# Column sums of three weight groups on GpSimd, one mean product each, and another order of the opening's splits and statistics

## The chip, the cores and the metric

The kernel runs on one core of one Trainium2 chip. A core has a matrix engine (TensorE; PE in the profile, its weight loads PEld), three engines that work element by element (VectorE = DVE, ScalarE = ACT, GpSimd = POOL) and a queue engine (SyncE = SP) that issues most of the transfers between the chip's memory and the core's on-chip memory, SBUF. Products are summed in PSUM, in eight banks. Each engine works through its own list of instructions in order and waits at semaphores for the others. The metric is the device time of one execution in microseconds; lower is better.

## The reference, cut to what matters

```python
x = A_u                                   # 1 x 2048 x 448, float32
g = sigmoid((x * gate_w).sum(-1))         # a gate per token
a = s4d_convolution(x, ...) + x * D_skip  # branch A
# branch B: a shift mixer, then an MLP
h  = gelu(layernorm(x) @ w1)              # 448 x 448
hs = shifted_by_1_-1_2_-2(h) @ w2         # four channel groups of 112, each shifted along the tokens
x1 = x + hs
b  = x1 + gelu(layernorm(x1) @ w3) @ w4   # 448 -> 1792 -> 448
out = g * a + (1 - g) * b
```

Only `layernorm(x) @ w1` for the first 512 tokens, and what follows from it, is touched by the change. The layernorm is rewritten: `layernorm(x) @ w1 = r * (x @ (w1 - column means of w1))`, where `r` is one over the standard deviation of a token. So the kernel subtracts from every column of `w1` that column's mean over the 448 inputs, multiplies, and scales the result by `r` afterwards.

## The kernel before, in words

The 2048 tokens are cut into 4 blocks of 512 (`NB`, `TB`). A unit is one group of output channels for one block: 16 units of kind "a" (the mixer; per block the four 112-channel groups of `w1`, in the order 0, 2, 1, 3), then 56 of kind "d" (the MLP; 14 per block). A unit has a first product `first(n)` into a PSUM bank, an activation, and a second product `second(n)` that adds into four banks `acc0` to `acc3`, one for each 128 tokens.

All products are in float32 by splitting: a value is a rounded high part (`xh`, `w1h`, `w2h`, `uh`), made by a ScalarE copy, and a low part (`xl`, `w1l`, `w2l`, `ul`), made by a VectorE subtraction. A product is then three: high by high, high by low, low by high. A `first` has 11 matmuls (four 128-row pieces of the 448 inputs, the last of which holds 64 high and 64 low rows), a `second` has 12.

The order of all work is written by hand: inside `tc.manual_schedule()` each engine does its instructions in the order in which the code calls them. `begin()` (line 780) is the opening: everything from the start up to the second product of unit 3. After it comes a loop over the units with tables of what is done at which unit.

What the opening calls:

- `constants()` fills small tiles on GpSimd, among them `cm`, a column of 1/448. `first_loads()` issues the transfers: `w1` group 0 and group 2 on ACT's queue, `x` of the first block (`x0`, a left and a right half of the 512 tokens), group 1, the rows of `x` for the statistics, then group 3, and later the identity `idt`, `w2` and the next block on SP's queue.
- `warm_up(m)` issues `m` products of zeros on TensorE.
- `presum(0)` gives the means of group 0: VectorE adds pieces 0 and 1 of the group into `ws`, and three float32 products with the broadcast column `cm` (64 rows of piece 3, piece 2, then `ws`) leave the mean of every column in a bank `pm`, the same in all 128 partitions. `col_means(g)` does it for the groups 2, 1 and 3 with four products and no addition, the fourth over the 64 rows of piece 3. A float32 product shows as two records in the profile.
- `center(g)` subtracts `pm` from the weights `w1r` in place (VectorE); `hi(*s1(g))` and `lo_(*s1(g))` then split them into `w1h` and `w1l`; `s2(g)` stands for the same of `w2`.
- `x_hi`, `x_lo` split the first block's `x`: `lh` is its left half, `rh` its right; `split_hi(1, ...)`, `split_lo(1, ...)` those of the second block. `c0`, `c1` are the left and right 256 output columns of unit 0.
- `stats_act(j)`, `stats_b(j0, j1)` give mean and variance of 128 tokens on ScalarE or VectorE; `rstd` is eleven short VectorE instructions from the variance to `r1`; `rstd_rows` transposes `r1` on TensorE (one product for each 128 tokens) and copies it to the rows `rb` on ScalarE.
- `act_mul(n)` (VectorE) scales unit n by `rb`; `act_head(n)` (ScalarE) is the GELU and the copy `uh`; `act_tail(n)` (VectorE) gives `ul`.

Of the kernel before, what the change touches and what calls it, by code (L numbers as in the profile page):

```python
# [17 lines left out]
D = 448  # L18
# [156 lines left out]
def mixer_and_small_steps(ctx, tc, xs, gg, okm, x, xT, xb, x0, w1, w2, w3, w4, par, logdt, dskip, ident, out):  # L175
# [9 lines left out]


    idt = big.tile([128, 128], F32, name="idt")
    cm = big.tile([128, 1], F32, name="cm")
    rt = big.tile([128, 1], F32, name="rt")
    rb = wk.tile([128, L + 2 * HALO + 8], F32, name="rb", tag="rb", bufs=1)  # L190
    warm = big.tile([128, 2 * TB], mybir.dt.bfloat16, name="warm", tag="yt")
# [77 lines left out]

    def constants():  # L270
        nc.gpsimd.memset(warm[:, :TB], 0.0)
        nc.gpsimd.memset(cm, 1.0 / D)
        nc.gpsimd.memset(one, 1.0)
        nc.gpsimd.memset(nu, 0.0)
        nc.gpsimd.memset(zero, 0.0)
        nc.gpsimd.memset(carry, 0.0)
        nc.gpsimd.memset(rb[:, 0:HALO], 0.0)
        nc.gpsimd.memset(rb[:, L + HALO:L + 2 * HALO], 0.0)
# [201 lines left out]
    def second(n):  # L480
        kind, b, i = units[n]
        if kind == "a":
            wh, wl, m = w2h[:, i, :], w2l[:, i, :], G
            s, e = i == 0, i == 3
        else:
            wh, wl = W4[i]
            m = 128
            s, e = i == 0, i == NF - 1
        for j in range(NT):
            if s:  # L490
                ACC[j] = ps.tile([128, D], F32, name=f"acc{j}", tag=f"acc{j}", bufs=1)
        q = [(j, p) for p in range(3) for j in range(NT)]
        if s or e:
            q.sort()
        for j, p in q:
            t = slice(j * 128, (j + 1) * 128)
            nc.tensor.matmul(ACC[j], (UL if p == 2 else UH)[n][:m, t], wl if p == 1 else wh,  # L497
                             start=s and p == 0, stop=e and p == 2)
# [197 lines left out]
        return pm[g]  # L696


    def col_means(g):
        p = mean_bank(g)  # L700
        for k in range(4):
            r = 64 if k == 3 else 128
            nc.tensor.matmul(p, cm[:r].to_broadcast([r, 128]), w1r[:r, g, k, :G],  # L703
                             start=(k == 0), stop=(k == 3))

    w4p, w3r = {}, {}

# [25 lines left out]
        for _ in range(m):  # L733
            nc.tensor.matmul(pw, warm[:, 0:128], warm[:, :TB], start=True, stop=True)  # L734

    def presum(g, m=1):

        t = big.tile([128, G], F32, name="ws", tag="lt")
        a, p = w1r[:, g, :, :G], mean_bank(g)
        nc.vector.tensor_add(t, a[:, 0, :], a[:, 1, :])  # L740
        if m > 1:
            nc.vector.tensor_add(t, t, a[:, 2, :])
        if m > 2:
            nc.vector.tensor_add(t[:64], t[:64], a[:64, 3, :])
        q = ((64, a[:64, 3, :]), (128, a[:, 2, :]))[:3 - m] + ((128, t),)
        for k, (r, q_) in enumerate(q):
            nc.tensor.matmul(p, cm[:r].to_broadcast([r, 128]), q_, start=(k == 0), stop=(k == 3 - m))  # L747

    def center(g, k0=0, k1=4):
        t = w1r[:, g, k0:k1, :G]  # L750
# [6 lines left out]
    def lo_(h, lo, src):  # L757
        nc.vector.tensor_tensor(lo, src, f32(h), OP.subtract)
# [21 lines left out]
    def begin():  # L780
        constants()
        first_loads()
        nc.scalar.activation(rt, cm, AF.Gelu_apprx_tanh)
        hl_tiles(("a", 0))
        warm_up(8)
        x_hi(0, lh)
        presum(0)
        center(0, 0, 2)
        center(0, 2, 4)
        warm_up(4)  # L790
        hi(*s1(0, 0, 2))
        x_lo(0, 2, lh)
        hi(*s1(0, 2, 4))
        x_hi(2, lh)
        first(0, seq=[(0, x_, k, *c0) for x_ in range(2) for k in range(2)], stop=False)
        col_means(2)
        lo_(*s1(0))
        first(0, seq=[(1, 0, k, *c0) for k in range(2)], stop=False)
        x_lo(3, 4, lh)
        x_lo(2, 3, lh)  # L800
        first(0, seq=[(w, 0, k, *c0) for k in (2, 3) for w in range(2)] + [(0, 1, 2, *c0)], stop=False)
        center(2)
        x_hi(2, rh)
        x_hi(0, rh)
        x_lo(3, 4, rh)
        hi(*s1(2))
        x_lo(2, 3, rh)
        first(0, seq=[(w, 0, k, *c1) for k in (2, 3, 0, 1) for w in range(2)], stop=False)
        x_lo(0, 2, rh)
        first(0, seq=[(0, 1, k, *c1) for k in (2, 0, 1)])  # L810
        col_means(1)
        lo_(*s1(2))
        first(1, seq=wh_wl)
        center(1)
        stats_act(2)
        stats_act(3)
        hi(*s1(1))
        stats_b(0, 2)
        col_means(3)
        stats_b(NT, NT + 1)  # L820
        hi(*s2(0))
        split_hi(1, 0, 2)
        first(2, seq=wh_wl[:7], stop=False)
        rstd(r1, 0, NT + 1)
        center(3)
        hi(*s1(3))
        rstd_rows(0, NT, "acc1")
        lo_(*s1(1))
        first(2, seq=wh_wl[7:])
        first(3, "misc", wh_wl[:7], stop=False)  # L830
        act_mul(0)
        lo_(*s1(3))
        first(3, seq=wh_wl[7:])
        lo_(*s2(0))
        act_head(0)
# [182 lines left out]
```

## Time and profile before

| what | value |
|---|---|
| three timed runs | 381.64, 382.9 and 383.3 us, median 382.9 |
| span of the profiled execution | 381.7 us |
| TensorE weight loads, busy | 318.3 us, 83% |
| VectorE busy | 294.9 us, 77% |
| ScalarE busy | 210.2 us, 55% |
| GpSimd, first work after the constants | at 49.08 us |
| 14 to 20 us: TensorE, VectorE, ScalarE busy | 6.00, 4.77, 2.99 of 6.00 us |
| 20 to 27 us: the same | 6.92, 5.12, 5.76 of 7.00 us |
| 38 to 93 us: the same | 54.45, 44.93, 29.76 of 55.00 us |

Times are counted from the start of the profiled execution, whose own time is its span with a little before and behind it that the profile does not hold. TensorE is busy nearly all the time, so its short gaps matter, and among them those in the first 40 us, where the change lies. In the chain of waits a piece of TensorE means that the engine had work in its list without a wait; a piece of another engine means that something waited for that.

### The profile page before, as it was taken

What the parts mean: (1) busy time and instruction counts of PE and PEld (TensorE: products, weight loads), DVE (VectorE), ACT (ScalarE), POOL (GpSimd) and SP (SyncE); (2) the same over time, 40 slices, a digit from 0 to 9 for tenths busy, and PEclk for the clock granted to TensorE, in tenths of its full rate; (3) what the DMA queues carried; (4) which work ended last, traced back from release to release, by engine and by line L of the source; (5) the groups of instructions that cost most, each with busy time, mean ns of one, the idle gap of its engine ahead of it and who ended that gap; (6) DMA issues with size and microseconds to landing.
All of it is one profiled execution on the core that took longest, in us unless ns stands there. A gap on an engine that the chain in (4) does not pass through costs nothing.

```text
span 381.7 us, 5198 instructions
## 1 busy us (share of the span) xinstructions
PE 373.2 (98%) x1728; PEld 318.3 (83%) x1728; DVE 294.9 (77%) x527; ACT 210.2 (55%) x349; POOL 65.3 (17%) x176
## 2 busy tenths in 40 slices
PE   8999999999999999999999999999999999999993
PEld 4878888887888888888888888888888888888882
DVE  3679988785866992888389999999788999995312
ACT  4575646636878566743275576465756745442220
POOL 1000061412000000030022536334142440000000
PEclk9999999999999999999999999999999999999998
DMA  8934505354724409000762614355785212271202
GB/s 268 371 99 184 193 29 154 48 102 142 257 87 128 73 16 216 32 0 0 194 131 43 117 28 106 95 173 110 108 186 152 60 21 35 57 198 31 82 0 101
DMA packets 85896, 42.26 MB, mean 111 GB/s; under 512 B 67030, under 2 KB 80614, under 8 KB 85226
## 3 DMA queue, kind: packets, MB, share of 16 engines
q1 hardware_dynamic: 85434, 41.20, 41.8%
q10 hardware_dynamic: 432, 0.70, 0.6%
q8 instruction: 15, 0.25, 0.3%
q14 instruction: 15, 0.12, 0.1%
HBM read 30.86 MB, written 11.02 MB: 110 GB/s over the span
## 4 chain that ended last, share of the span: by engine, by line
PE 92%; DVE 2%; DMA 2%; SPq 1%; ACT 0%; issue 0%; POOL 0%; DVEq 0%; POOLq 0%
PE p L435 45%; PE acc L497 44%; DMA raw<-w_in 2%; PE pw L734 1%; PE pm L703 1%; SPq L398 1%; DMA xd<-xt 1%; PE pm L747 0%; DVE b L284 0%; PE misc L334 0%; DVE w1r L751 0%; DVE w3l L218 0%; SPq L395 0%; DVE uf L444 0%; DVE ul L470 0%
## 5 line engine op out<-in xcount | busy, mean ns | idle before, releaser
L457 ACT ACTIVATE uf<-p 128x512 f32<-128x512 f32 x56 | 33.4, 597 | 102.9 <-PE p L435 102.9
L470 DVE TENSOR_TENSOR ul<-uf,uh 128x512 fp32r<-128x512 f32 (+1 forms) x72 | 48.8, 680 | 32.9 <-ACT uh L466 32.8
L620 DVE TENSOR_TENSOR_SCAN z<-z,carry 128x512 f32<-128x512 f32 x48 | 61.4, 1280 | 3.7
L435 PE MATMUL p<-xh,w3l 128*128 128x512 f32 x224 | 61.0, 393 | 0.6 <-DVE w3l L218 0.6
L435 PE MATMUL p<-xh,w3h 128*128 128x512 f32 x224 | 61.3, 396 | 0.0
L497 PE MATMUL acc<-w4h,uh 128*128 128x448 f32 x224 | 58.2, 364 | 0.0
L497 PE MATMUL acc<-w4h,ul 128*128 128x448 f32 x224 | 58.1, 364 | 0.0
L497 PE MATMUL acc<-w4l,uh 128*128 128x448 f32 x224 | 58.1, 363 | 0.0
L435 PEld LDWEIGHTS p<-xh,w3l 128*128 128x128 f32 x224 | 42.0, 188 | 10.8 <-DVE w3l L218 1.0
L435 PE MATMUL p<-xl,w3h 128*128 128x512 f32 x168 | 48.0, 394 | 0.0
L435 PEld LDWEIGHTS p<-xh,w3h 128*128 128x128 f32 x224 | 42.0, 188 | 6.7
L497 PEld LDWEIGHTS acc<-w4h,uh 128*128 128x128 f32 x224 | 42.0, 188 | 6.1
L466 ACT ACTIVATE uh<-uf 128x512 fp32r<-128x512 f32 (+1 forms) x72 | 45.5, 633 | 2.3
L497 PEld LDWEIGHTS acc<-w4l,uh 128*128 128x128 f32 x224 | 42.0, 188 | 3.2
L497 PEld LDWEIGHTS acc<-w4h,ul 128*128 128x128 f32 x224 | 42.0, 188 | 3.1
L615 ACT ACTIVATE z<-zs,nu 128x512 f32<-128x512 f32 x64 | 42.2, 709 | 0.7 <-DMA zs<-xT_in 0.7
L435 PEld LDWEIGHTS p<-xl,w3h 128*128 128x128 f32 x168 | 31.6, 188 | 7.2
L614 POOL COPY z<-carry 128x1 f32<-128x1 f32 x48 | 34.5, 731 | 17.2 <-DVE zs L626 17.1
L321 POOL TENSOR_TENSOR t<-r 128x4 f32<-128x4 f32 (+1 forms) x15 | 5.7, 377 | 149.1 <-DVE r L319 148.3
L622 POOL COPY carry<-z 128x1 f32<-128x1 f32 x48 | 14.2, 295 | 91.4 <-DVE z L620 89.8
L454 ACT ACTIVATE uf<-uf 112x512 f32<-112x512 f32 x16 | 10.1, 630 | 22.6 <-DVE uf L444 22.5
L620 DVE TENSOR_TENSOR_SCAN z<-z,carry,zero 128x512 f32<-128x512 f32 x16 | 20.0, 1247 | 0.0
(136 smaller groups left out, 488.8 us busy)
## 6 DMA issues: line engine op xcount, KB each, us to landing
zs<-xT_in SPq DMA_DIRECT2D x4, 1024.0 KB, 8.2
yd<-yt SPq DMA_DIRECT2D x56, 64.0 KB, 2.0
ysb<-yd SPq DMA_DIRECT2D x16, 224.0 KB, 2.6
out_dram<-xs SPq DMA_DIRECT2D x16, 224.0 KB, 2.4
raw<-xb_in SPq DMA_DIRECT2D x3, 1032.0 KB, 5.8
raw<-w_in SPq DMA_DIRECT2D x3, 1024.0 KB, 5.3
xd<-xt SPq DMA_DIRECT2D x16, 192.0 KB, 2.1
xr<-xd SPq DMA_DIRECT2D x16, 192.0 KB, 3.7
```

What stands on the lines that cost most here:

```text
L321: eng.tensor_mul(t, y, y)
L398: nc.sync.dma_start(p[o:o + 64, 3, :].rearrange("p (t c) -> p t c", c=32), d[384 * 128:].rearrange("(g p c) -> p g c", p=64, c=32))
L435: nc.tensor.matmul(p[:m, t0:t1], (wl if w else wh)[:, k, :], (xl if x_ else xh)[:, k, o + t0:o + t1], start=(q == 0 and fresh), stop=stop ...
L454: nc.scalar.activation(UF[n][:m], UF[n][:m], AF.Gelu_apprx_tanh)
L457: nc.scalar.activation(UF[n][:m], P1[n][:m], AF.Gelu_apprx_tanh)
L466: nc.scalar.activation(UH[n][:m], UF[n][:m], AF.Copy)
L470: nc.vector.tensor_sub(UL[n][:m], UF.pop(n)[:m], f32(UH[n][:m]))
L497: nc.tensor.matmul(ACC[j], (UL if p == 2 else UH)[n][:m, t], wl if p == 1 else wh, start=s and p == 0, stop=e and p == 2)
L614: nc.gpsimd.tensor_copy(z4[:, m, 0:1], carry[:, k, m:m + 1])
L615: nc.scalar.activation(z4[:, m, 1:], ZS[b][:, k, :], AF.Copy, scale=nu[:, k, m:m + 1])
L620: nc.vector.tensor_tensor_scan(z, z, up, carry[:, k, m:m + 1], OP.add, OP.add)
L622: nc.gpsimd.tensor_copy(carry[:, k, m:m + 1], z[:, TB - 1:])
```

## The change: what it does

```diff
-    cm = big.tile([128, 1], F32, name="cm")
+    cm = big.tile([128, 2], F32, name="cm")
...
-        nc.gpsimd.memset(cm, 1.0 / D)
+        nc.gpsimd.memset(cm[:, 0:1], 1.0 / D)
+        nc.gpsimd.memset(cm[:64, 1:2], 1.0 / D)
+        nc.gpsimd.memset(cm[64:, 1:2], 0.0)
...
         q = [(j, p) for p in range(3) for j in range(NT)]
-        if s or e:
+        if s and n or e:
             q.sort()
...
+    PS = []
+    def pool_sum(g):
+        if not PS:
+            PS.append(wk.tile([128, 4, G], F32, name="wsum", tag="u"))
+        t, a = PS[0][:, g], w1r[:, g, :, :G]
+        nc.gpsimd.tensor_add(t, a[:, 0, :], a[:, 1, :])
+        nc.gpsimd.tensor_add(t, t, a[:, 2, :])
+        nc.gpsimd.tensor_add(t[:64], t[:64], a[:64, 3, :])
+
     def col_means(g):
-        p = mean_bank(g)
-        for k in range(4):
-            r = 64 if k == 3 else 128
-            nc.tensor.matmul(p, cm[:r].to_broadcast([r, 128]), w1r[:r, g, k, :G],
-                             start=(k == 0), stop=(k == 3))
+        nc.tensor.matmul(mean_bank(g), cm[:, 0:1].to_broadcast([128, 128]), PS[0][:, g], start=True, stop=True)
...
-    def presum(g, m=1):
+    def presum():
         t = big.tile([128, G], F32, name="ws", tag="lt")
-        a, p = w1r[:, g, :, :G], mean_bank(g)
+        a, p = w1r[:, 0, :, :G], mean_bank(0)
         nc.vector.tensor_add(t, a[:, 0, :], a[:, 1, :])
...
-        q = ((64, a[:64, 3, :]), (128, a[:, 2, :]))[:3 - m] + ((128, t),)
-        for k, (r, q_) in enumerate(q):
-            nc.tensor.matmul(p, cm[:r].to_broadcast([r, 128]), q_, start=(k == 0), stop=(k == 3 - m))
+        for q, (c, r) in enumerate(((1, a[:, 3, :]), (0, a[:, 2, :]), (0, t))):
+            nc.tensor.matmul(p, cm[:, c:c + 1].to_broadcast([128, 128]), r, start=q == 0, stop=q == 2)
...
     def begin():
         constants()
         first_loads()
...
         warm_up(8)
         x_hi(0, lh)
-        presum(0)
+        presum()
+        for g in (2, 1, 3):
+            pool_sum(g)
+        x_hi(2, lh)
+        x_lo(0, 2, lh)
+        warm_up(3)
         center(0, 0, 2)
         center(0, 2, 4)
-        warm_up(4)
         hi(*s1(0, 0, 2))
-        x_lo(0, 2, lh)
         hi(*s1(0, 2, 4))
-        x_hi(2, lh)
-        first(0, seq=[(0, x_, k, *c0) for x_ in range(2) for k in range(2)], stop=False)
-        col_means(2)
-        lo_(*s1(0))
-        first(0, seq=[(1, 0, k, *c0) for k in range(2)], stop=False)
         x_lo(3, 4, lh)
         x_lo(2, 3, lh)
-        first(0, seq=[(w, 0, k, *c0) for k in (2, 3) for w in range(2)] + [(0, 1, 2, *c0)], stop=False)
+        first(0, seq=[(0, x_, k, *c0) for x_ in range(2) for k in range(2)], stop=False)
+        lo_(*s1(0))
+        first(0, seq=[(0, 0, 2, *c0), (0, 0, 3, *c0), (0, 1, 2, *c0)] + [(1, 0, k, *c0) for k in range(4)], stop=False)
+        col_means(2)
         center(2)
...
-        first(0, seq=[(w, 0, k, *c1) for k in (2, 3, 0, 1) for w in range(2)], stop=False)
+        first(0, seq=[(w, 0, 2, *c1) for w in range(2)] + [(w, 0, k, *c1) for k in (0, 1, 3) for w in range(2)], stop=False)
         x_lo(0, 2, rh)
         first(0, seq=[(0, 1, k, *c1) for k in (2, 0, 1)])
+        lo_(*s1(2))
         col_means(1)
-        lo_(*s1(2))
         first(1, seq=wh_wl)
         center(1)
         stats_act(2)
+        hi(*s1(1))
         stats_act(3)
-        hi(*s1(1))
         stats_b(0, 2)
+        lo_(*s1(1))
         col_means(3)
         stats_b(NT, NT + 1)
-        hi(*s2(0))
-        split_hi(1, 0, 2)
-        first(2, seq=wh_wl[:7], stop=False)
-        rstd(r1, 0, NT + 1)
         center(3)
         hi(*s1(3))
+        split_hi(1, 0, 2)
+        hi(*s2(0))
+        first(2, seq=wh_wl)
+        rstd(r1, 0, NT + 1)
+        first(3, "misc", wh_wl[:7], stop=False)
         rstd_rows(0, NT, "acc1")
-        lo_(*s1(1))
-        first(2, seq=wh_wl[7:])
-        first(3, "misc", wh_wl[:7], stop=False)
+        rstd_rows(NT, NT + 1, "acc2")
+        lo_(*s1(3))
         act_mul(0)
-        lo_(*s1(3))
         first(3, seq=wh_wl[7:])
...
         second(0)
-        rstd_rows(NT, NT + 1, "p1")
         act_mul(2)
```

Three things change in the list of the engines. On TensorE, in the stretch from the means of group 1 to the second product of unit 0 (`p_202`, `p_240`, `p_274` are the banks of units 1, 2 and 3, `misc` that of the transposes of `r_82`, which is `r1`), there stood before:

```order
L703 MATMUL pm<-w1r,cm 128x112 x4
L435 MATMUL p_202<-xh,w1h 112x512 x4
L435 MATMUL p_202<-xl,w1h 112x512 x3
L435 MATMUL p_202<-xh,w1l 112x512 x4
L435 MATMUL p_240<-xh,w1h 114x512 x4
L435 MATMUL p_240<-xl,w1h 114x512 x3
L334 MATMUL misc<-idt,r_82 128x128 x4
L435 MATMUL p_240<-xh,w1l 114x512 x4
L435 MATMUL p_274<-xh,w1h 112x512 x4
L435 MATMUL p_274<-xl,w1h 112x512 x3
L435 MATMUL p_274<-xh,w1l 112x512 x4
L497 MATMUL acc_309<-w2h,uh 128x448
```

The same stretch in the changed kernel, where the three banks are called `p_207`, `p_245` and `p_270`:

```order
L713 MATMUL pm<-wsum,cm 128x112
L437 MATMUL p_207<-xh,w1h 112x512 x4
L437 MATMUL p_207<-xl,w1h 112x512 x3
L437 MATMUL p_207<-xh,w1l 112x512 x4
L437 MATMUL p_245<-xh,w1h 114x512 x4
L437 MATMUL p_245<-xl,w1h 114x512 x3
L437 MATMUL p_245<-xh,w1l 114x512 x4
L437 MATMUL p_270<-xh,w1h 112x512 x4
L437 MATMUL p_270<-xl,w1h 112x512 x3
L336 MATMUL misc<-idt,r_82 128x128 x5
L437 MATMUL p_270<-xh,w1l 112x512 x4
L499 MATMUL acc_314<-w2h,uh 128x448
```

Each group's four mean products are one (that of group 3 stands between units 1 and 2 in both), and the transposes stand behind seven matmuls of unit 3, no longer behind seven of unit 2; the fifth transpose, which came after `second(0)`, has joined the four.

On VectorE, the stretch from the low part of group 2's weights to the scaling of unit 0 (`b` and `st` are the statistics, `w1r<-w1r,pm` is `center`) was before:

```order
L758 TENSOR_TENSOR w1l<-w1r,w1h 128x456
L751 TENSOR_TENSOR w1r<-w1r,pm 128x4x112
L284 BN_STATS b_222<-xs 128x6 x2
L286 BN_AGGR st<-b_222 128x2 x2
L284 BN_STATS b_232<-xs 128x6
L286 BN_AGGR st<-b_232 128x2
L299 TENSOR_SCALAR v<-st 128x5
...
L308 SCALAR_TENSOR_TENSOR r_82<-t,r_82 128x5
L751 TENSOR_TENSOR w1r<-w1r,pm 128x4x112
L758 TENSOR_TENSOR w1l<-w1r,w1h 128x456
L444 TENSOR_TENSOR uf<-p_158,rb 112x512
```

and is now:

```order
L762 TENSOR_TENSOR w1l<-w1r,w1h 128x456
L755 TENSOR_TENSOR w1r<-w1r,pm 128x4x112
L286 BN_STATS b_227<-xs 128x6 x2
L288 BN_AGGR st<-b_227 128x2 x2
L762 TENSOR_TENSOR w1l<-w1r,w1h 128x456
L286 BN_STATS b_235<-xs 128x6
L288 BN_AGGR st<-b_235 128x2
L755 TENSOR_TENSOR w1r<-w1r,pm 128x4x112
L301 TENSOR_SCALAR v<-st 128x5
...
L310 SCALAR_TENSOR_TENSOR r_82<-t,r_82 128x5
L762 TENSOR_TENSOR w1l<-w1r,w1h 128x456
L446 TENSOR_TENSOR uf<-p_171,rb 112x512
```

The low part of group 1 and the centering of group 3 have moved ahead of the eleven instructions of `rstd`.

GpSimd had nothing to do between its constants and the instructions of the later `rstd`; it now has, behind the constants (`ISA` sets up the engine):

```order
L280 MEMSET rb 128x2
L708 ISA
L708 TENSOR_TENSOR wsum<-w1r 128x112
L709 TENSOR_TENSOR wsum<-wsum,w1r 128x112
L710 TENSOR_TENSOR wsum<-wsum,w1r 64x112
```

and the same three additions twice more, for groups 1 and 3: nine additions that came from nowhere, in place of nine TensorE products.

More of the change, by code (lines that the diff above doesn't have):

```diff
@@ L734, in warm_up @@
             nc.tensor.matmul(pw, warm[:, 0:128], warm[:, :TB], start=True, stop=True)
-    def presum(g, m=1):
+    def presum():
         t = big.tile([128, G], F32, name="ws", tag="lt")
-        a, p = w1r[:, g, :, :G], mean_bank(g)
+        a, p = w1r[:, 0, :, :G], mean_bank(0)
         nc.vector.tensor_add(t, a[:, 0, :], a[:, 1, :])
[L741 to L744, printed above, removed]
-        q = ((64, a[:64, 3, :]), (128, a[:, 2, :]))[:3 - m] + ((128, t),)
-        for k, (r, q_) in enumerate(q):
-            nc.tensor.matmul(p, cm[:r].to_broadcast([r, 128]), q_, start=(k == 0), stop=(k == 3 - m))
+        for q, (c, r) in enumerate(((1, a[:, 3, :]), (0, a[:, 2, :]), (0, t))):
+            nc.tensor.matmul(p, cm[:, c:c + 1].to_broadcast([128, 128]), r, start=q == 0, stop=q == 2)
     def center(g, k0=0, k1=4):
@@ L782, in begin @@
         first_loads()
-        nc.scalar.activation(rt, cm, AF.Gelu_apprx_tanh)
+        nc.scalar.activation(rt, cm[:, 0:1], AF.Gelu_apprx_tanh)
         hl_tiles(("a", 0))
```

## The prediction

> **What bounds the kernel now.** I read the page's busy shares first, then the chain of work that ended last, then the opening in order of time.
>
> ```profile
> PE 373.2 (98%) x1728; PEld 318.3 (83%) x1728; DVE 294.9 (77%) x527; ACT 210.2 (55%) x349; POOL 65.3 (17%) x176
> PE 92%; DVE 2%; DMA 2%; SPq 1%; ACT 0%; issue 0%; POOL 0%; DVEq 0%; POOLq 0%
> ```
>
> TensorE is the bound. All that is changed lies before 28 us, and no transfer is moved past another. The chain there, and the one later place where it leaves TensorE:
>
> ```profile
> 9.29 1.65 PE pm L703 x8
> ...
> 13.66 1.07 PE pm L703 x8
> ...
> 14.75 0.62 DVE w1r L751
> ...
> 20.20 0.55 DVE w1l L758
> ...
> 20.79 3.71 PE p L435 x15
> ...
> 40.33 2.53 PE p L435 x11
> ...
> 75.52 0.34 PE misc L334 x3
> ...
> 92.67 1.42 PE p L435 x5
> ```
>
> From 14.75 to 20.79 the chain runs over VectorE while TensorE is busy too: the two are level, so TensorE's time alone isn't what the change can win. The stall before 92.67 follows a TensorE transpose at 75.52, so it moves with it: what the opening wins by 38 us reaches the end.
>
> **The change, part by part.** The rows of the opening:
>
> ```profile
> 4.83 1.46 PE L747 MATMUL pm<-w1r,cm 64*128 64x112 f32 x4
> 6.09 0.64 PE L747 MATMUL pm<-ws,cm 128*128 128x112 f32 x2
> 6.52 1.92 PE L734 MATMUL pw<-warm 128*128 128x512 bf16 x4
> 8.66 0.63 PE L435 MATMUL p<-xl,w1h 128*114 128x256 f32 x2
> 9.08 1.86 PE L703 MATMUL pm<-w1r,cm 128*128 128x112 f32 x8
> 10.98 0.62 DVE L751 TENSOR_TENSOR w1r<-w1r,pm 128x448 f32<-128x448 f32 x1 [1.46 <-PE pm L703]
> 11.63 0.42 DVE L776 TENSOR_TENSOR xh<-raw,xh 64x256 fp32r<-64x256 f32 x1
> 12.08 1.03 DVE L778 TENSOR_TENSOR xl<-raw,xh 128x256 fp32r<-128x256 f32 x2
> 13.03 0.63 DVE L758 TENSOR_TENSOR w1l<-w1r,w1h 128x456 fp32r<-128x456 f32 x1
> 14.64 1.18 PE L435 MATMUL p<-xh,w1h 128*112 128x512 f32 x4
> 17.28 1.22 PE L703 MATMUL pm<-w1r,cm 128*128 128x112 f32 x8
> 18.43 1.17 PE L435 MATMUL p<-xh,w1h 128*114 128x512 f32 x4
> ```
>
> 1. *Group 0's means.* Six half products lie between 4.83 and 6.52, 1.69 us. Two of 128 rows start 0.21 apart (6.09, then 6.52 after two). Six without 64-row passes: 1.29. Gain 0.4. One warm-up product less: four start in 8.44 - 6.52 = 1.92, about 0.43 each with the last one's tail taken off. Unit 0's first product, two ahead of 8.66 and so at 8.23, comes at 8.23 - 0.83 = 7.4 to 7.5.
>
> 2. *Group 2's mean.* It came after 4 products of unit 0; now it comes after 11, at 0.21 each (two from 8.66 to 9.08): 7.45 + 2.3 = 9.8. It is then 2 half products, not 8 (1.86). `center(2)`, which waits for it, starts at about 10.45 where it started at 10.98: 0.5 earlier. Its four followers on VectorE (11.63 to 13.66) are the same, so the last of unit 0's products, which need them, end 0.5 earlier too.
>
> 3. *Groups 1 and 3.* The mean of group 3 takes 18.43 - 17.28 = 1.15 for 8 half products; one product is 0.22. Gain 0.93, twice. `first(1)`, at 14.64, starts at 13.2; `first(2)`, at 18.43, at about 15.95.
>
> 4. *The transposes.* These now stand behind 18 matmuls from there, 0.23 each (11 in 2.53): 15.95 + 4.14 = 20.1. Where they stood:
>
> ```profile
> 19.50 0.17 DVE L308 SCALAR_TENSOR_TENSOR r<-t,r 128x5 f32<-128x5 f32 x1
> 20.11 0.60 PE L334 MATMUL misc<-idt,r 128*128 128x128 f32 x4
> 20.75 0.60 ACT L335 ACTIVATE rb<-misc 128x512 f32<-128x512 f32 x1
> 21.45 0.69 DVE L444 TENSOR_TENSOR uf<-p,rb 112x512 f32<-112x512 f32 x1 [0.71 <-ACT rb L335]
> 22.18 0.63 ACT L454 ACTIVATE uf<-uf 112x512 f32<-112x512 f32 x1 [0.83 <-DVE uf L444]
> 24.35 0.36 PE L497 MATMUL acc<-w2h,uh 112*128 112x448 f32 x1
> 26.30 0.63 ACT L466 ACTIVATE uh<-uf 112x512 fp32r<-112x512 f32 x1
> 26.98 1.07 PE L497 MATMUL acc<-w2h,uh 112*128 112x448 f32 x4
> 27.38 0.69 DVE L444 TENSOR_TENSOR uf<-p,rb 112x512 f32<-112x512 f32 x1 [0.72 <-ACT rb L335]
> 28.73 0.70 PEld L497 LDWEIGHTS acc<-w2h,ul 112*128 112x128 f32 x4 [0.24 <-DVE ul L470]
> 37.26 0.41 PEld L334 LDWEIGHTS misc<-idt,r 128*128 128x128 f32 x4 [0.35 <-DVE r L308]
> ```
>
> They started at 20.11. The saving has been spent on 11 more matmuls ahead of them: the transposes don't move. `r1` was ready at 19.67; its chain starts 1.35 earlier now (center(1)) and has two 0.55 us pieces more ahead of it: 19.4, so TensorE decides, not VectorE.
>
> 5. *What waits for them.* The scaled unit 0 and its GELU keep their times, 21.45 and 22.18, so `uh` is ready at about 23.5. TensorE has only 4 more matmuls and the fifth transpose, and is done at 21.5 (20.1, 0.55 and 0.92). `second(0)` starts at 23.5, not 24.35, behind a **new gap of 2.0 us**. It takes 2.4 and ends at 25.9. `second(1)` needs unit 1's `uh`, the copy at 26.30, ready at 26.93; ScalarE's list between `rb` and that copy is full and unchanged but for the fifth row of `rb`, which lies in a wait. So `second(1)` starts at 26.9 as before, behind a **second gap of 1.0 us**. Of 3 us won on TensorE nothing is left here but 0.05.
>
> 6. *What remains.* The fifth transpose no longer stands ahead of the scaling of unit 2: its wait of 0.72 at 27.38 goes, and with it the 0.24 at 28.73. ScalarE's later work follows up to 0.7 earlier, and most of the wait at 37.26 (0.35, on the weight side, about 0.1 of the stream) goes. Together 0.3 to 0.4. The new order of `second(0)` lets its low part come later, which nothing needs.
>
> 7. *GpSimd's sums.* The trace has no such addition. Rows near it:
>
> ```profile
> w1r<-w_in ACTq DMA_DIRECT2D x1, 228.0 KB, 5.3
> 0.73 0.52 POOL L271 MEMSET warm<- 128x512 bf16 x1 [0.29 <-POOLq L1010]
> 49.73 0.20 POOL L322 TENSOR_TENSOR t<-t,v 128x4 f32<-128x4 f32 x1
> 53.04 0.69 DVE L470 TENSOR_TENSOR ul<-uf,uh 112x512 fp32r<-112x512 f32 x1
> 53.21 1.78 POOL L321 TENSOR_TENSOR t<-r 128x4 f32<-128x4 f32 x1 [0.49 <-DVE r L319]
> 53.64 1.29 DVE L361 TENSOR_TENSOR xl<-raw,xh 128x516 fp32r<-128x516 f32 x2
> ```
>
> An addition of 4 elements takes 0.20; a fill of 512 takes 0.52, about 0.8 ns an element. With two inputs and an output over 112 elements that is 0.20 to 0.48; I take 0.48, the upper end. Below it is bounded by 0.20, above by the 1.78 that one took while VectorE ran three subtractions of two SBUF inputs without a break (53.04 to 54.93): it ended when they did. In the opening, group 2 lands 5.3 us after its issue at 1.17, at 6.5. One addition fits in before VectorE's run of `x_lo`, `x_lo`, `lo_(0)`, which begins at 7.1 and lasts 1.5 (0.42, 0.5 and 0.63); the other two follow it, and the sum is there at 9.6. TensorE comes for it at 9.8: covered, by 0.2. Group 1's sum follows at 9.7 to 11.3; its last addition meets VectorE's next run at 11.1 and costs that 0 to 0.2. Without this cover each 0.1 later is 0.1 on the path up to the transposes. Group 3's has a gap of more than a microsecond.
>
> The Trainium skill, in "SBUF — State Buffer", section "Who interferes with whom", says that a VectorE instruction with two SBUF inputs and a GpSimd one that reads SBUF exclude each other, and that the one that started first holds the port to its end. The trace agrees (the 1.78 above). The sum is the same by rule and row, except that by the rule a VectorE split can also wait for an addition, at most the 0.48 that I have counted.
>
> Sum: -0.05 (second(1)) - 0.35 (after it) + 0 to 0.2 (sums) = **-0.2 us** against the profiled execution, 381.7 to 381.5. This execution lies 1.2 under the median of the runs, so the median goes from 382.9 to **382.7 us**. By measurement that is no change: runs of this kernel can tell about 0.5%, 1.9 us.
>
> **The rivals.**
>
> *GpSimd is the bound (slower).* Place: the mean product of group 2 or 1, which now heads TensorE's list; everything behind waits. Point: an addition of 0.6 us. Then group 2's third ends at 9.9, group 1's last just misses the gap before VectorE's run at 11.2 and waits for its end at 13.3: the mean of group 1 comes 1.1 late, and about 0.8 is left at the end. At 0.8 an addition it is 2.4 late and +2.0. For it: the margin is 0.2 and 53.21 shows starvation. Against it: 0.48 is already the upper reading of the rows. Time 383.7 to 384.9.
>
> *The first GpSimd addition pays for a start (slower).* The first one in the trace came 47 us after the engine was last busy, so its code had all that time to load; here it has 5. From rows, one late first addition of 1.6 (1.78 - 0.20) puts group 2's sum at 9.8 to 10.2 and costs 0.1 to 0.5. The Trainium skill, in "GPSIMD Engine Reference", section "Instruction dispatch", puts the first call after a load at some 6 us; an estimate by that page, if the 6 us began only with the first addition, is +3.3 us, 386.2, and no run here shows it.
>
> *The fast clock comes earlier (faster).* At first TensorE runs at half pace: a half product takes 0.21 in the 6.09 row and 0.15 in the 17.28 row, a pass of 512 columns 0.43 in the 6.52 row and 0.23 later. The step lies between the 9.08 and the 14.64 row, and the change leaves fewer holes between 4.8 and 6.5. If that opens the clock a few microseconds sooner, the 11 products take 1.3 less, group 2's mean is then held by its sum at 9.6, and about 0.9 is won on the transposes: 381.6.
>
> *All TensorE work that is taken out counts.* 0.4 + 0.43 + 1.4 + 0.93 + 0.93 = 4.1: 378.8. For it: 98% busy. Against it: the two gaps of part 5, which hang on VectorE and ScalarE.
>
> **How the numbers follow.** Forecast (-1.0 to +0.5): 0.50. GpSimd the bound 0.21, half of it over 1.9. A late first addition 0.07, most of it over 1.9. Clock 0.16, a quarter over 1.9. All counts 0.06. So faster 0.12, same 0.68, slower 0.20. The likeliest case alone reaches from 381.9 to 383.4; the range reaches to the priced ends of the GpSimd and clock rivals: 380.8 to 385.2.
>
> **What would show it.** Right: TensorE idle for about 2 us before unit 0's second product and 1 us before unit 1's, released by ScalarE's `uh`; the transposes within 0.5 of 20.1; the second product of unit 1 within 0.5 of 26.9; each mean product two records of 0.2 to 0.4 with no wait. Wrong: a wait of TensorE on a `wsum`; additions of over 0.6; `center(2)` later than 10.98; the transposes released by `r1`; the first passes at full pace well before 9; a gain at 27 us that is lost by 93.

## The result, and the profile after

| | before | after |
|---|---|---|
| median of 22 runs each, us | 382.85 (381.1 to 383.67) | 382.6 (382.06 to 384.05) |
| span of the profiled execution, us | 381.7 | 381.7 |
| TensorE weight loads busy, us | 318.3 | 315.8 |
| GpSimd busy, us | 65.3 | 69.2 |

The ratio of the times, after to before, is 1.001 with a 95% interval of 0.9997 to 1.0023: no change that can be measured, as forecast. (It isn't the quotient of the two medians, which is 0.9993.) The time of a run is its span and about 1.8 us. The page of the changed kernel, busy shares and the chain that ended last:

```profile
PE 370.4 (97%) x1709; PEld 315.8 (83%) x1709; DVE 294.9 (77%) x527; ACT 210.1 (55%) x349; POOL 69.2 (18%) x187
...
PE 90%; DVE 3%; ACT 2%; DMA 1%; issue 1%; SPq 1%; POOL 0%; DVEq 0%; POOLq 0%
```

TensorE has 19 records fewer and is busy 2.8 us less, and the end does not move: its share of the chain fell from 92 to 90%. The opening of the changed kernel on TensorE, in order of time (start, duration, then what; in brackets the idle time before and what ended it):

```profile
7.37 0.49 PE L437 MATMUL p<-xh,w1h 128*114 128x256 f32 x2
...
9.40 0.37 PE L713 MATMUL pm<-wsum,cm 128*128 128x112 f32 x2
...
19.45 0.71 PE L336 MATMUL misc<-idt,r 128*128 128x128 f32 x5
...
22.79 1.07 PE L499 MATMUL acc<-w2h,uh 112*128 112x448 f32 x4 [1.70 <-ACT uh L468]
23.70 1.64 PE L499 MATMUL acc<-w2l,uh 112*128 112x448 f32 x4
25.14 1.70 PE L499 MATMUL acc<-w2h,ul 112*128 112x448 f32 x4
26.63 1.21 PE L499 MATMUL acc<-w2h,uh 112*128 112x448 f32 x4
27.68 0.96 PE L499 MATMUL acc<-w2l,uh 112*128 112x448 f32 x4
...
92.11 0.72 PE L437 MATMUL p<-xh,w3l 128*128 128x512 f32 x2 [0.52 <-DVE w3l L218]
```

Unit 0's second product stands behind a gap of 1.70 us, as forecast. Four of its passes then take 1.64 to 1.70 us where four take 0.96 to 1.07 elsewhere. The same two stretches in the view by windows (length; busy time and count of PE, PEld, DVE, ACT, POOL; granted clock; DMA share; GB/s):

```profile
20.33:23.74 3.41, 1.71 (x9) 1.15 (x8) 2.20 (x4) 2.74 (x6) 0.00 (x0) 1.00 0.03 5
23.74:27.16 3.42, 3.42 (x11) 3.03 (x10) 2.88 (x6) 3.39 (x7) 0.00 (x0) 0.50 0.60 158
```

After a window that TensorE filled by half, the granted clock fell to 0.50 for the length of one more window. Still, the row at 92.11, the first product after the stall that all profiles have there, comes 0.56 before its place in the profile of before (92.67). This lead is gone later. VectorE in that stretch, and the chain of waits there (start, length, what):

```profile
286.98 0.56 DVE L373 TENSOR_TENSOR xl<-xr,xh 128x384 fp32r<-128x384 f32 x1 [2.15 <-ACT xh L406]
...
289.12 0.56 DVE L373 TENSOR_TENSOR xl<-xr,xh 128x384 fp32r<-128x384 f32 x1 [1.26 <-ACT xh L406]
```

```profile
305.08 2.54 PE p L437 x11
...
310.10 1.29 DVE z L622
...
312.10 0.68 DVE xs L508
...
312.91 2.67 PE acc L499 x12
```

Ahead of the splits of block 3, whose data come back from the chip's memory, VectorE waited 3.4 us (1.8 in the profile of before: 0.98 and 0.85) and ran late from there; at 312 us a second product needs `acc0`, which VectorE's `xs` has yet to read, and TensorE stands idle for 0.34 us. So three things have to be told apart: what the new means win, what the new order costs, and what the rest of the kernel lets through.

### The profile page after: what moved, and what is told of

The parts are those of the page before. It is cut to its first block, busy times and chain, and to the rows that moved or that the text cites. A ratio compares the mean times of both kernels' runs of the same rounds, so it can differ in the third digit from the quotient of the medians.

```text
span 381.7 us, 5172 instructions
## 1 busy us (share of the span) xinstructions
PE 370.4 (97%) x1709; PEld 315.8 (83%) x1709; DVE 294.9 (77%) x527; ACT 210.1 (55%) x349; POOL 69.2 (18%) x187
## 4 chain that ended last, share of the span: by engine, by line
PE 90%; DVE 3%; ACT 2%; DMA 1%; issue 1%; SPq 1%; POOL 0%; DVEq 0%; POOLq 0%
PE p L437 45%; PE acc L499 44%; PE pw L743 1%; DMA xr<-xd 1%; DMA xd<-xt 1%; ACT uh L468 0%; PE misc L336 0%; PE pm L751 0%; DVE uf L446 0%; DVE xl L782 0%; DVE xs L508 0%; DVE z L622 0%; SPq L400 0%; ACT uf L456 0%; ACT lr L524 0%
## 5 line engine op out<-in xcount | busy, mean ns | idle before, releaser
L499 PE MATMUL acc<-w2h,uh 112*128 112x448 f32 x64 | 19.3, 371 | 1.7 <-ACT uh L468 1.7
```

## The experiments

"Row at 92" is the first product after the stall of 92.67 (before) and 92.11 (after), in each kernel's profile: what the opening has won by then.

| kernel | unit 1's second product, us | row at 92, us | ratio to before (95% interval) |
|---|---|---|---|
| before, first profile | 26.98 | 92.67 | |
| before, third profile | 25.07 | 90.79 | |
| the changed kernel, second profile | 26.21 | 91.60 | 1.0015 (0.9997 to 1.0033) |
| new means, old order | 24.27 | 90.06 | 0.9972 (0.9952 to 0.9992) |
| old means, new order | 29.50 | 94.83 | 1.0083 (1.0052 to 1.0113) |
| group 0's means alone | 25.18 | 90.90 | 0.9986 (0.9968 to 1.0004) |
| changed, transposes early | 25.52 | 90.91 | 0.9986 (0.9967 to 1.0005) |
| changed, gap filled | 26.46 | 91.87 | 1.0005 (0.9985 to 1.0025) |
| changed, twice the additions | 27.31 | 92.69 | 1.0079 (1.0051 to 1.0107) |

The profiles differ by more than the edits: in that of the old means in the new order the clock was at 0.50 from 26.02 to 29.43 us, and the first one of before had a late clock (both below).

### Means and order apart

The kernel before with the new means alone: the two-column `cm`, `presum`, `pool_sum` and the one-product `col_means` of the change, ahead of the old list of the opening.

```diff
         presum()
+        for g in (2, 1, 3):
+            pool_sum(g)
```

> The kernel before with only the new means: three sums on GpSimd, one product each, group 0 without 64-row passes; the old order of splits, statistics and transposes. Theory 1 (the new means win time, the new order spends it): transposes released by r1 at 18.3 to 18.7 instead of 20.1, unit 0's scaling 1.2 to 1.8 earlier, unit 1's second product at 25.6 to 26.2 instead of 27.0; 1.0 to 1.5 us faster than the kernel before, 381.3 to 381.9. Rival 1 (the new order is needed for the win, VectorE's chain center(1), statistics, r1, center(3) binds as much as TensorE): r1 ready no earlier than 19.2, less than 0.5 faster, 382.3 to 382.9. Rival 2 (the additions stand in the way of VectorE's old order): a wait of TensorE on a sum or VectorE splits more than 0.5 late, time 383.0 to 384.

And the changed kernel's list with the old means, four products for each of three groups, and no sums:

```diff
-        for g in (2, 1, 3):
-            pool_sum(g)
+        presum(0)
```

> The changed kernel with the old means (four float32 products for each of the groups 2, 1 and 3, group 0 with 64-row passes) and no sums on GpSimd, in the new order. Theory 1 (the new order by itself is later, since the transposes stand behind eleven more matmuls): transposes at 21.5 to 23, unit 1's second product at 27.5 to 29, time 1.0 to 2.5 above the kernel before, 383.8 to 385.3. Rival (the order by itself is neutral or better, and the new means give nothing): within 0.4 of the kernel before.

TensorE in the kernel with the new means alone, in order of time:

```profile
8.51 0.47 PE L713 MATMUL pm<-wsum,cm 128*128 128x112 f32 x2 [0.51 <-POOL wsum L710]
...
17.16 0.62 PE L336 MATMUL misc<-idt,r 128*128 128x128 f32 x4 [0.67 <-issue]
18.19 1.16 PE L437 MATMUL p<-xh,w1l 128*114 128x512 f32 x4 [0.41 <-DVE w1l L762]
...
21.74 0.36 PE L499 MATMUL acc<-w2h,uh 112*128 112x448 f32 x1
...
24.27 1.07 PE L499 MATMUL acc<-w2h,uh 112*128 112x448 f32 x4
...
90.06 0.74 PE L437 MATMUL p<-xh,w3l 128*128 128x512 f32 x2 [0.53 <-DVE w3l L218]
```

and in the kernel with the new order alone:

```profile
21.99 0.71 PE L336 MATMUL misc<-idt,r 128*128 128x128 f32 x5
...
25.40 1.36 PE L499 MATMUL acc<-w2h,uh 112*128 112x448 f32 x4 [1.77 <-ACT uh L468]
```

In the old order TensorE reaches the transposes at 17.16 and goes from 18.19 to the end of unit 1's second product without a gap. Both the transposes and that product (24.27) are earlier than expected (18.3 and 25.6 at the earliest); this execution had its full clock from 5.55 us, that of the prediction's rows from 10.49. The medians are 381.42 us against 381.61 of the kernel before on the same chip, and by the ratio 0.28% is won, 1.1 us. The new order with the old means loses 0.83%, 3.2 us: more than expected, with the transposes at 21.99, the gap of 1.77 behind them, and a low clock in three of the seven executions. So the means win and the order spends it. The two parts don't simply add: in the new order the new means win 0.0083 - 0.0010, some 2.8 us, in the old order 1.1. The one wait on a sum (0.51, ahead of 8.51) is in the old order, where TensorE comes for group 2's at 8.0; in the new it comes at 9.40.

### The transposes' place, and the gap

The changed kernel with both `rstd_rows` ahead of the seven matmuls of unit 3:

```diff
-        first(3, "misc", wh_wl[:7], stop=False)
         rstd_rows(0, NT, "acc1")
         rstd_rows(NT, NT + 1, "acc2")
+        first(3, "misc", wh_wl[:7], stop=False)
```

> The changed kernel with the five transposes of r1 ahead of the seven matmuls of unit 3, not behind them. Theory 1 (the time won on TensorE is lost because the transposes wait behind eleven more matmuls): the transposes start when r1 is ready, at 18.5 to 18.7 instead of 19.45, unit 0's second product at about 21.9 instead of 22.8, the gap ahead of it shrinks by at least 0.8, unit 1's second product follows ScalarE and comes 0.6 to 0.9 earlier; median 381.7 to 382.0, less where the clock no longer drops. Rival (the opening is held by ScalarE's list, not by the place of the transposes): rows early, but unit 1's uh still at 25.5 and its second product at 26.2 to 26.6, median 382.4 to 382.7.

TensorE, and ScalarE's list ahead of unit 1's `uh`, in that kernel:

```profile
18.70 0.73 PE L336 MATMUL misc<-idt,r 128*128 128x128 f32 x5 [0.62 <-PE p L437]
...
22.07 1.07 PE L499 MATMUL acc<-w2h,uh 112*128 112x448 f32 x4
...
25.52 1.07 PE L499 MATMUL acc<-w2h,uh 112*128 112x448 f32 x4 [0.77 <-ACT uh L468]
```

```profile
22.66 1.16 ACT L358 ACTIVATE xh<-raw 128x516 fp32r<-128x516 f32 x2
23.72 0.56 ACT L759 ACTIVATE w2h<-w2r 112x448 fp32r<-112x448 f32 x1
24.19 0.61 ACT L456 ACTIVATE uf<-uf 112x512 f32<-112x512 f32 x1
24.83 0.63 ACT L468 ACTIVATE uh<-uf 112x512 fp32r<-112x512 f32 x1
```

The gap ahead of unit 0's second product is gone, and the row at 92 comes 0.69 before its place in the changed kernel (91.60); 381.58 us, ratio 0.9986. Theory 1 holds, and the rival has a part: ScalarE starts the `uh` of unit 1 at 24.83 behind a list that has no hole since 20.72, so the second gap stays (0.77).

Then the gap was filled with products of zeros:

```diff
         first(3, seq=wh_wl[7:])
+        warm_up(8)
         lo_(*s2(0))
```

> The changed kernel with eight products of zeros (128x512, bf16) on TensorE in the gap ahead of unit 0's second product, and nothing else. Theory 1 (TensorE's idle time before that product lets the clock drop for one stretch of 3.4 us, 23.7 to 27.2 us in the profile of the changed kernel): the granted clock stays at 1.00 from 20 to 28 us, unit 0's second product starts at the same time (22.8, at most 0.3 later) but its passes are 0.2 to 0.25 apart instead of 0.45, unit 1's second product starts when its uh is there (26.2 to 26.6) and runs at full pace; the runs above 383.0 us disappear and the median falls by 0.4 to 0.8 to about 382.0. Rival (the drop at 23.7 has nothing to do with the gap, or costs nothing because ScalarE's uh sets the time): the clock still drops in some executions, median within 0.2 of 382.6.

Half of it came. None of 12 executions had a mean granted clock of 0.993 or less (7 of the first 22 of the changed kernel had), and passes keep their pace. By itself this doesn't show that the zeros did it, since the next 12 executions of the changed kernel had none either. And the median was 382.56, not 382.0. TensorE in its profile:

```profile
21.27 1.67 PE L743 MATMUL pw<-warm 128*128 128x512 bf16 x7
23.09 1.05 PE L499 MATMUL acc<-w2h,uh 112*128 112x448 f32 x4
...
26.46 1.08 PE L499 MATMUL acc<-w2h,uh 112*128 112x448 f32 x4 [0.72 <-ACT uh L468]
```

The zeros end at 22.94, and unit 0's second product comes 0.3 later, at 23.09; 0.11 of that was there at the transposes (19.56 for 19.45). The row at 92 is at 91.87. The changed kernel itself once more:

> The changed kernel itself once more, so that the others of this call stand beside it on one chip. Theory 1 (TensorE's gap lets the clock drop for one stretch in some executions): about a third of its executions have a mean granted clock of 0.993 or less and take 1.0 to 1.5 us more than the rest; the rest lie at 382.0 to 382.7; ratio to the kernel before 1.001 to 1.003. Rival (the drop was a single accident): no execution at 0.993 or less.

```profile
7.31 0.49 PE L437 MATMUL p<-xh,w1h 128*114 128x256 f32 x2 [1.15 <-ACT w1h L759]
...
19.43 0.71 PE L336 MATMUL misc<-idt,r 128*128 128x128 f32 x5
...
22.77 1.07 PE L499 MATMUL acc<-w2h,uh 112*128 112x448 f32 x4 [1.70 <-ACT uh L468]
...
26.21 1.07 PE L499 MATMUL acc<-w2h,uh 112*128 112x448 f32 x4 [0.77 <-ACT uh L468]
...
91.60 0.73 PE L437 MATMUL p<-xh,w3l 128*128 128x512 f32 x2 [0.52 <-DVE w3l L218]
```

This is TensorE in its profile: the same gap of 1.70, and the clock stayed. The expectation of a third failed: none of these 12 was at 0.993 or less. In a variant that leaves the opening as it is (the moved scans, below) 6 of 12 were, and these took 0.3 us more on average than the other six. The two profiles of one kernel price the drop: 92.11 with it, 91.60 without, 0.5 us. I had put it at 1.0 to 1.5, from the seven executions with a low clock (383.03 to 384.05 us) beside the rest (382.06 to 382.65, but for two of 383.15 and 383.24). What else made the first seven long isn't settled.

### GpSimd's margin

```diff
-        nc.gpsimd.tensor_add(t, a[:, 0, :], a[:, 1, :])
+        for _ in range(4):
+            nc.gpsimd.tensor_add(t, a[:, 0, :], a[:, 1, :])
```

> The changed kernel with three more GpSimd additions for each of the three sums (the first addition is done four times, which changes no value). Theory 1 (the sums are hidden: group 2's was ready at 7.94 us and TensorE came for it at 9.40): three more at 0.45 us put it at 9.3 to 9.6, TensorE waits 0 to 0.3 for it, the sums of groups 1 and 3 stay in time, and the whole is 0 to 0.4 us slower than the changed kernel. Rival 1 (GpSimd is the bound): each addition counts, 1.0 to 1.4 us slower. Rival 2 (the additions cost through VectorE, which waits behind them): VectorE's three subtractions between 7.1 and 8.9 us come 0.4 or more later each, center(2) at 10.5 or later, 0.6 or more slower with no wait of TensorE on a sum.

First the additions of group 2 in the changed kernel, then GpSimd and the weight loads' waits with three more for each sum:

```profile
6.53 0.38 POOL L708 TENSOR_TENSOR wsum<-w1r 128x112 f32<-128x112 f32 x1 [4.70 <-DMA w1r<-w_in]
6.99 0.42 POOL L709 TENSOR_TENSOR wsum<-wsum,w1r 128x112 f32<-128x112 f32 x1
7.49 0.45 POOL L710 TENSOR_TENSOR wsum<-wsum,w1r 64x112 f32<-64x112 f32 x1
```

```profile
6.53 1.84 POOL L709 TENSOR_TENSOR wsum<-w1r 128x112 f32<-128x112 f32 x4 [4.70 <-DMA w1r<-w_in]
...
9.01 0.65 POOL L711 TENSOR_TENSOR wsum<-wsum,w1r 64x112 f32<-64x112 f32 x1
```

```profile
9.47 0.51 PEld L437 LDWEIGHTS p<-xh,w1l 128*114 128x114 f32 x4 [0.60 <-DVE w1l L763]
...
11.72 0.17 PEld L437 LDWEIGHTS p<-xh,w1h 128*114 128x114 f32 x1 [0.80 <-DVE xh L781]
...
13.07 0.28 PEld L437 LDWEIGHTS p<-xl,w1h 128*114 128x114 f32 x2 [0.61 <-DVE xl L783]
```

Rival 2 was right. Group 2's sum was there at 9.66 and TensorE came at 10.05: no wait on a sum, as nowhere in the changed kernel, where that sum was there at 7.94 and asked for at 9.40. TensorE waits longer for VectorE's splits instead (0.60, 0.80 and 0.61 us; 0.37, 0.66 and 0.43 in the changed kernel), which are held up behind the additions: the two `xl` of the right half took 1.32 us here and 1.03 there. The row at 92 comes 1.09 later than in the second profile of the changed kernel. Not all of this is due to the additions: unit 0's first product was already 0.35 late (7.66 for 7.31), and VectorE's first addition, ahead of any of GpSimd's, had waited for the weights until 5.05 (4.50). That leaves about 0.74 for nine more additions, 0.08 each. The median, 385.1, is 2.3 above the changed kernel's on the same chip; three of these six executions had a clock of 0.992 or less, and what the other 1.2 are isn't settled.

### The clock of the kernel before

Group 0's means without 64-row passes, and nothing else of the change:

```diff
-            nc.tensor.matmul(p, cm[:r].to_broadcast([r, 128]), q_, start=(k == 0), stop=(k == 3 - m))
+            nc.tensor.matmul(p, cm[:, c:c + 1].to_broadcast([128, 128]), r, start=q == 0, stop=q == 2)
```

> The kernel before with one part of the change alone: group 0's means without a 64-row pass (a column of cm that is zero in the lower 64 rows). Theory 1 (a small gain of 0.4 us on the chain to center(0), which the later waits of the opening mostly keep): the first product of unit 0 0.3 to 0.5 earlier for the same opening of the clock, 0 to 0.4 us faster, ratio 0.999 to 1.000, and the executions spread as those of the kernel before (3 us). Rival (the 64-row passes hold the clock back: the kernel before opened it at 10.5 us, the changed one at 6.7): the clock opens before 8 us, the executions above 382.5 us go, 0.5 to 1.0 us faster.

The median was 381.60 against 382.18, ratio 0.9986. By the record of the granted clock it opened (rose to its full pace) at 5.69 us, and no execution of 12 was above 382.22, where 10 of the 29 of the kernel before beside it were above 382.9 (25 of 82 above 382.6 over three chips, 12 of 22 in the first comparison). So the rival was right on the spread, and the size, 0.5 to 0.6 us, lies in its range, though the interval of the ratio reaches 1.0004. The kernel before once more, unchanged:

> The kernel before once more, for a second look at when its clock opens. Theory (its first means leave the clock's opening to chance: 10.5 us in the first profile, while seven profiles of kernels without that stretch, or with another phase, opened it at 4.4 to 6.8): if its own time is under 382 us the clock opens before 8 us and the first product of unit 1 stands near 13.5 instead of 14.64; if it is above 383 us, near 10 us again. Rival (the spread of the kernel before has nothing to do with the opening of the clock): time and opening don't go together.

It took 383.24, the clock opened at 10.20 and unit 1's first product stood at 14.54. And a third time:

> The kernel before a third time; its two profiled executions so far took 383.46 and 383.24 us and opened the clock at 10.5 and 10.2 us. Theory (the time of the kernel before goes with the opening of its clock): if this execution is under 382.4 us, the clock opens before 8 us, unit 0's means of group 2 run at full pace and unit 1's second product starts 1 us or more before 26.9; if it is over 382.9, the clock opens near 10 us again. Rival (the spread comes from elsewhere): an execution under 382.4 with the clock open only at 9 to 10.5 us, or one over 382.9 with it open before 8.

This one took 381.67 and opened its clock at 5.16. Its TensorE rows:

```profile
7.80 1.22 PE L703 MATMUL pm<-w1r,cm 128*128 128x112 f32 x8
...
18.20 0.60 PE L334 MATMUL misc<-idt,r 128*128 128x128 f32 x4
...
25.07 1.08 PE L497 MATMUL acc<-w2h,uh 112*128 112x448 f32 x4
...
90.79 0.73 PE L435 MATMUL p<-xh,w3l 128*128 128x512 f32 x2 [0.57 <-DVE w3l L218]
```

The means of group 2 take 1.22 us where the prediction's row had 1.86, and everything from unit 1's second product on is 1.9 earlier. The three profiles of the kernel before agree with the theory in both directions: the profile that the prediction was read from is one of the executions with the late clock. Beside the one with the early clock the changed kernel, at 26.21 for unit 1's second product, is 1.1 late, and 0.8 late at 92 us.

### Where the rest of the kernel lets it through

With the new means VectorE's list behind `r1` is next, so its order was tried: the low part of group 1 ahead of `center(3)`, the rows' copy ahead of group 3's high part.

```diff
+        lo_(*s1(1))
+        rstd_rows(0, NT, "acc1")
         center(3)
         hi(*s1(3))
-        rstd_rows(0, NT, "acc1")
-        lo_(*s1(1))
```

> The kernel before with the new means, in the old order but for one step: behind the statistics the low part of group 1 comes ahead of center(3) on VectorE, and the copy of the transposed rows ahead of the high part of group 3 on ScalarE. Theory 1 (with the new means VectorE's list behind r1 sets TensorE's time, and what stands in it decides): the wait of 0.41 us before the last matmuls of unit 2 goes, the scaling of unit 0 comes 0.4 to 0.5 earlier, unit 0's second product at 21.2 to 21.4 instead of 21.74; 0.3 to 0.5 us faster than the kernel with the new means alone, less if the second product of block 3's first unit near 311 us takes it back: ratio to the kernel before 0.995 to 0.997. Rival (TensorE's list sets it, or the later stretch near 311 us takes back all that the opening still wins): unit 0's second product earlier, end within 0.2 us of the kernel with the new means alone, ratio 0.997 to 0.998.

A miss in the opening: the wait of 0.41 went, but a weight load now waits 0.55 for group 3's high part, and unit 0's second product starts at 21.70 (21.74). The ratio is 0.9971 (0.9953 to 0.9989), that of the new means alone. Both of these profiles lose about 0.9 us of their lead near 312. So the scans there were moved ahead of the splits that wait for the transfer, in the changed kernel and in this one:

```diff
-                ssm_some(n, 3.9 - (2.2 if units[n][2] == NF - 1 else 0.0) - spent)
+                ssm_some(n, 3.9 + {52: 2.5, 53: -2.5}.get(n, 0.0) - (2.2 if units[n][2] == NF - 1 else 0.0) - spent)
```

> The changed kernel with two of VectorE's scans of the convolution moved ahead of the splits of block 3 near 285 us, where VectorE waited 2.15 and 1.26 us for a transfer (the opening is untouched). Theory (what the opening still wins, 0.6 to 0.8 us at 93 us, is taken back near 312 us, where the second product waits for VectorE, which is late by its waits near 285 us): the waits ahead of the splits shrink by 2 us or more, VectorE's xs at 312 us comes 1 us or more earlier, no step back of the second products at 312 us; 0.4 to 0.9 us faster than the changed kernel, about 382.0, and fewer executions above 383 us. Rival (TensorE's lead is lost to something else, or the scans only move the wait): the second product near 312 us still 0.5 late, within 0.2 of the changed kernel.

> The same move of two scans in the kernel with the new means, the old order and the low part of group 1 ahead of center(3). Theory: its second products are 2.65 us ahead of the profile before up to 305 us and 1.77 ahead from 312 us on; with the scans moved the 0.9 stay: 0.6 to 1.0 us faster than without the move, ratio to the kernel before 0.994 to 0.996. Rival (the floor near 312 us is set by the transfer itself, not by VectorE's order): the lead falls to 1.8 there again, ratio 0.997.

VectorE near 285 us in the changed kernel with the scans moved:

```profile
287.69 0.53 DVE L373 TENSOR_TENSOR xl<-xr,xh 128x384 fp32r<-128x384 f32 x1
...
289.50 0.56 DVE L373 TENSOR_TENSOR xl<-xr,xh 128x384 fp32r<-128x384 f32 x1 [0.96 <-ACT xh L406]
```

and the chain of waits near 312 us in the kernel with the means, the swap and the scans moved, without a piece of VectorE:

```profile
308.00 2.54 PE p L437 x11
310.54 2.44 PE acc L499 x12
312.97 2.54 PE p L437 x11
```

By the profiles the floor was VectorE's order: the waits of 3.4 us in the changed kernel are 1.0, although the second split ran later than without the move (289.50 for 289.12), and no lead is lost in either profile (2.6 us ahead of the first profile of before at 92 us and at the end in the second kernel, where without the move it fell to 1.8). That kernel is the fastest here: 380.84 us against 382.01, ratio 0.9964 (0.9948 to 0.9979), 1.4 us faster than the kernel before. The times show less of the move itself: 0.994 to 0.996 was expected, and 0.9964 lies within the interval of the same kernel without it (0.9971). In the changed kernel the move gave less than I expected: 382.58, ratio 1.0006 (0.9990 to 1.0021), within the interval of the changed kernel's own 1.0015; two of 12 executions were above 383 us, four of 12 without the move. That the move wins time is thus seen in the profiles and not shown by the times.

## Why the prediction was right, and where it was not

The forecast of no measurable change holds; the median is within 0.1 us of it. The runs could tell more than the 0.5% that the prediction allowed them: the interval is 0.13% to either side. By its steps:

1. *Group 0's means.* Unit 0's first product at 7.37 (7.4 to 7.5 forecast). The number is right, but in part by luck: it was not the sum on TensorE that set it. Its weights waited for ScalarE's `w1h`, which stood behind the copy of `x`. In the second profile, where TensorE had nothing left to do from 6.16 on, the product still came only at 7.31 (the wait of 1.15).
2. *Group 2's mean.* At 9.40 (9.8), `center(2)` at 9.81 (10.45). The step that failed is the durations: rows of the prediction's profile from before 10 us were of an execution whose clock opened at 10.5. In the changed kernel it opened at 6.7, so the 11 products ran at full pace. This is the rival of the earlier clock; I gave it 0.16, and its price of 0.9 on the transposes measured 0.66. One link of it was other: the 11 products took 2.03 us, only 0.3 less than forecast where the rival had 1.3, because TensorE's weight loads waited between them for VectorE's low parts (0.16 and 0.37 us). These held group 2's mean, not its sum.
3. *Groups 1 and 3.* Right: a mean product holds TensorE for 0.13 to 0.14 us in place of 1.15, a gain of 1.0 each for 0.93. In the forecast of unit 2's start is a slip: its own terms give 18.43 - 0.5 - 2 x 0.93 = 16.07, not 15.95. It came at 15.23.
4. *The transposes don't move, and TensorE decides.* Who decides was right: `r1` was ready at 18.52, the transposes started at 19.45, and moving them alone won 0.7 us. That they don't move was wrong by those 0.66.
5. *The gaps.* 1.70 in both profiles for 2.0, and 0.77 in the second for 1.0, both ended by `uh`: right. The clock's drop was not foreseen; it costs 0.5 us by the profiles where it happens, and in the first profile its slow passes filled the second gap.
6. *What remains.* The lead at 92 us was 0.56 and 1.07 in two profiles, for 0.2 to 0.4. But "what the opening wins by 38 us reaches the end" failed: I looked for waits after 38 us in a profile that had no lead, where the wait near 312 us doesn't show. Between 92 and 318 us the two profiles of the changed kernel lost 0.6 and 1.2.
7. *GpSimd's sums.* 0.37 to 0.45 an addition for 0.48, but for the first one of group 3, which took 0.73 beside a VectorE split (above the 0.6 that the prediction named as a sign of being wrong; nothing waited for it). Group 2's sum came at 7.94, not 9.6: its additions did not have to wait for the whole of VectorE's run. Where the two met, either could be the one that waits: in the second profile an addition took 0.65 us, and a split `w1l` 0.81 in place of 0.62. The rival of the bound GpSimd is out: the price of more additions was paid on VectorE. The rival of a late start is out too: the first addition took 0.38 us at 6.53, when its data had landed. The Trainium skill, "GPSIMD Engine Reference", section "Instruction dispatch", has some 6 us for a first call to freshly loaded code; the trace shows no such time behind 6.53, and whether it passed before, where GpSimd has no row from 1.8 us on, not even for the `ISA` in its list, can't be seen.

The base was off as well: "this execution lies 1.2 under the median" set a span beside times. With the 1.8 us around the span it took 383.5 and lay 0.6 above. So the right total is luck, two misses that cancel: more was won by 92 us than forecast, and more of it lost after. The base itself is a mixture: in the first comparison 12 of the 22 executions of before were above 382.6 us; beside the later runs, where fewer were, its median was 381.6 to 382.2, and the changed kernel stood at 382.77 beside 382.18. That all TensorE work counts is out: of 2.8 us less work in the profile, and some 4 by the rows, none arrived.

What the experiments show in its place: the new means are worth about 1.1 us in the old order (about half of it the end of the late clock, by two ratios whose intervals overlap), the new order costs 1.5 to 3.2 us, and in some executions VectorE's wait near 285 us takes back up to 1.2 of what is left.

## What to carry to other kernels

Work taken from the busiest engine is won only up to the next dependence: behind the last thing saved, ask who waits next (here for the transposes) and keep that early; how many products are gone says little. Look at more than one execution of the kernel before; a clock that opens late in, by their times, about a third of them makes the opening of one profile a bad ruler. And a lead is only as good as the later floors, which a profile without the lead cannot show.

## What was not expected of the hardware

The clock fell to half after a window that was half busy. In the changed kernel's profile it dropped from 23.74 to 27.16, one window of 3.41 us, after a window in which TensorE was busy for 1.71 of 3.41. The Trainium skill, "TensorE: Matmul & The Clock Gate", section "Part 1: The HAM clock gate (the "warmup" mystery)", speaks of an idle window of about 3.4 us that runs free of the kernel's start; length and free phase agree with the trace (the second profile, with the same gap, kept its clock), "idle" is too strong for these rows. Five profiles have a gap of 1.70 or 1.77 us at this place. Counted in stretches of 3.41 us from each one's opening of the clock, the three that dropped had TensorE busy for 1.64, 1.71 and 1.71 us in the stretch before; in the two that kept their clock the least busy stretch had 1.77 and 2.16. At the other end, the kernel before was busy on TensorE without a break from 3.4 to 6.8 us (3.40 of 3.40 in its first profile) and yet got its clock at 10.2 and 10.5 in two of three profiles. Without 64-row passes in group 0's means ten profiles got it at 4.4 to 6.8. In two profiles with them (the kernel before's third, and the new order alone) it came at 5.2 and 5.5; in the former the 3.41 us before hold products of zeros and only at their end, from 4.83 on, such a pass. That these passes count as half busy would explain all this, but it is a guess: no run tried it by itself.
